# Fused attention and gated MLP: clamping converted weights on GpSimd in the opening, with a reordered opening list

## The chip, the cores and the metric

The kernel runs on one core of one Trainium2 chip. The metric is device time in microseconds (us) of one execution; the number for a version is the median of several runs.

## The reference

Eight batches with eight heads, 576 rows, head width 64 and 32 memory slots go through an attention with a compressed memory. The 4608 x 512 result then goes through a gated MLP with 1536 hidden columns.

```python
a = exp(phi - max(phi, axis=2)); a = a / (sum(a, axis=2) + 1e-09)      # over the sequence
k_m = einsum('bhsm,bhsd->bhmd', a, k);  v_m = einsum('bhsm,bhsd->bhmd', a, v)
scores = scale * matmul(q, k_m^T);  attn = softmax(scores)            # over 32 slots
x = matmul(attn, v_m), heads side by side                             # 4608 x 512
out = (sigmoid(x @ w_gate) * (x @ w_val)) @ w_out
```

All three weights reach the kernel as 64-bit words of double precision numbers, and the kernel makes float32 of them itself.

## The kernel before

**Tiling.** The attention output x is never built. For each batch b and each of 12 hidden tiles f (128 columns of gate and of value), `u b f` multiplies the small memory `vT` by the weights of the tile, and `gate b f c` multiplies the result by the attention `at` of the batch. The halves c of a batch's sequence are 256 and 320 rows. `sig`, `mul` and the split into a high and a low part follow, and `out b f c` multiplies by w_out into four accumulators. Tiles f below 3 of batch 0 are plain float32, all other products take three float32r terms.

**Stages.** The work is a list of steps. The first twelve, batches 0, 1 and 2 with f from 0 to 3, are the opening; they also hold everything that must happen before the first gate. They are written out by hand as the string `OPENING`. Steps 12 and on run in loops that the change doesn't touch.

**What the list fixes.** `step` runs one task of the list, and `queued` puts what it issues on TensorE, VectorE, ScalarE and GpSimd behind the preceding task's instructions on the same engine. So the list is the issue order of each of these four queues. DMAs of the list go to SyncE's queue (SP) in list order, by `move`; only the writes of `leave` go to GpSimd's queue. An instruction that waits holds up all that is behind it on its engine.

**Tasks of the list.** `phi b`, `kvt b`, `kvm b g`, `q b c`, `words f k r` are loads (r is the room that takes the words; k=3 is a whole gate and value tile of 1 MB, k=0 and k=1 are its halves, k=2 is a w_out tile of 512 KB). `amax`, `aexp`, `asum` are the softmax over the sequence. The calls of `mem b` walk through twelve stages in order, whatever their second number is: transposes of g 0, copy, transposes of g 1, copy, transpose of the tail, copies, products with the keys and values of g 0 and of g 1, scaling, transposes, copy to `kT`, copy to `vT`. `scores`, `blocks`, `smax`, `sub`, `sexp`, `nsum`, `nmul`, `across`, `upper`, `lower` make the attention `at` in a high and a low part. `uhi`, `ulo`, `ghi`, `glo`, `wohi`, `wolo` split operands. `warm n` issues n products that nobody reads. `keep`, `again` store and reload `at`; `leave` moves out an accumulator.

**Conversion of the weights.** `mag f k` (line L267) lets ScalarE take the absolute value of the high words. `bits f k` then holds VectorE's four instructions: a clamp between TINY and HUGE (L273), a shift with a mask (L276), and two that put sign, exponent and low bits in (L280, L285). For k=3 each of the four has its own call of `bits`; for the others the first call holds two instructions and the second two. The opening has 14 such conversions, seven of 128x1024 elements and seven of 128x512. `table_of[0]` is set during the opening and None afterwards.

```python
nc.scalar.activation(dst, words_of[f, k][:, :, 1].bitcast(F32), AF.Abs)                  # mag
...
nc.vector.tensor_scalar(dst, dst, TINY, HUGE, op0=ALU.max, op1=ALU.min)                  # bits
if k == 3:
    yield
```

A room of `words` comes free at the last instruction of its `bits`, so that instruction releases the next load into it, and with it all that is behind this load in SP's queue. `phi 2` takes the buffer of `phi 0`.

Of the kernel before, what the change touches and what calls it, by code (L numbers as in the profile page):

```python
# [13 lines left out]
ALU = mybir.AluOpType  # L14
# [21 lines left out]
TINY, HUGE = 2.0**-15, 122879.9921875  # L36
# [22 lines left out]
nmul 0 1; sig 0 1 0; mem 1 6; bits 2 3; across 0 1; mem 2 2; mem 1 7; sig 0 0 0; words 3 2 1; bits 2 3;
gate 0 0 1; mul 0 1 0; bits 2 3; mem 1 8; sig 0 0 1; mag 0 2; q 1 1; mul 0 0 0; bits 0 2; u 0 2;  # L60
mem 1 10; bits 1 2; mem 1 9; scores 1 0; nospread; uhi 0 0 2; scores 1 1; words 3 3 2; mul 0 0 1;
gate 0 1 1; kvm 2 0; sig 0 1 1; uhi 0 1 2; blocks 1 0; mag 3 2; bits 0 2; bits 1 2; ghi 0 0 1; upper 0;
mag 3 3; blocks 1 1; wohi 1; smax 1; out 0 0 0; gate 0 2 1; words 2 2 0; bits 3 3; sub 1; bits 3 3;
sig 0 2 1; mem 2 0; gate 0 2 0; gleft 0 0 1; bits 3 3; mul 0 2 1; mem 2 5; kvm 2 1; mul 0 1 1;
sig 0 2 0; out 0 1 0; bits 3 3; out 0 0 1; mul 0 2 0; kvt 2; sexp 1; nsum 1; u 0 3; gleft 0 1 1;
ghi 0 1 1; nmul 1; mem 2 6; mem 2 11; ghi 0 2 1; uhi 0 0 3; out 0 1 1; uhi 0 1 3; ulo 0 0 3; across 1;
mem 2 7; mag 2 2; upper 1; lower 0; mem 2 8; ulo 0 1 3; lower 1; bits 2 2; bits 2 2; mem 2 10;
bits 3 2; wohi 0; gate 0 3 1; gate 0 3 0; gleft 0 2 1; u 1 0 1; q 2 0; mem 2 9; sig 0 3 1; out 0 2 0;
sig 0 3 0; scores 2 0; uhi 1 0 0 1; q 2 1; keep 0; out 0 2 1; mul 0 3 1; uhi 1 1 0 1; ulo 1 0 0 1;
bits 3 2; ulo 1 1 0 1; mul 0 3 0; wohi 3; scores 2 1; u 1 2 3; kvm 3 1; blocks 2 0; gleft 0 3 1;  # L70
ghi 0 3 0; gate 1 0 1; glo 0 3 0; wolo 3; kvm 3 0; ghi 0 3 1; blocks 2 1; glo 0 3 1; gate 1 0 0;
out 0 3 1; uhi 1 0 2 3; smax 2; words 4 3 0; sig 1 0 1; mul 1 0 1; sub 2; wolo 0; ghi 1 0 1; sig 1 0 0;
uhi 1 1 2 3; sexp 2; mul 1 0 0; gleft 1 0 1; leave 0 2; gate 1 1 1; wohi 2; gate 1 1 0; ulo 1 0 2 3;
ulo 1 1 2 3; ghi 1 0 0; nsum 2; glo 1 0 1; gate 1 3 0; sig 1 1 1; glo 1 0 0; sig 1 1 0; wolo 1;
mul 1 1 0; leave 0 3; sig 1 3 0; out 0 3 0; ghi 1 1 0; out 1 0 1; mul 1 1 1; gate 1 2 1; nmul 2;
ghi 1 1 1; mag 4 3; gleft 1 1 1; gate 1 2 0; leave 0 0; sig 1 2 1; again 0; bits 4 3; out 1 0 0;
words 4 2 2; leave 0 1; mag 4 2; glo 1 1 0; glo 1 1 1; across 2; bits 4 3; mul 1 2 1; ghi 1 2 1;
u 2 0 1; sig 1 2 0; uhi 2 0 0 1; keep 1; u 2 2 3; out 1 1 0; wolo 2; phi 3; mul 1 3 0; mul 1 2 0;
uhi 2 1 0 1; gate 1 3 1; ghi 1 2 0; bits 4 3; ulo 2 0 0 1; glo 1 2 1; upper 2; ulo 2 1 0 1; bits 4 3;
out 1 1 1; glo 1 2 0; bits 4 2; sig 1 3 1; lower 2; gleft 1 2 1; out 1 2 1; words 5 3 0; uhi 2 0 2 3;  # L80
mul 1 3 1; ulo 2 0 2 3; ghi 1 3 1; gate 2 0 1; bits 4 2; ghi 1 3 0; sig 2 0 1; glo 1 3 0; gate 2 0 0;
mag 5 3; glo 1 3 1; sig 2 0 0; mul 2 0 1; amax 3; out 1 2 0; mul 2 0 0; kvt 3; bits 5 3; bits 5 3;
bits 5 3; uhi 2 1 2 3; gate 2 1 0; ghi 2 0 1; gleft 2 0 1; ghi 2 0 0; out 1 3 1; out 1 3 0; glo 2 0 0;
words 6 3 1; ulo 2 1 2 3; sig 2 1 0; bits 5 3; gleft 1 3 1; mag 6 3; wohi 4; gate 2 3 1; gate 2 2 0;
bits 6 3; bits 6 3; gate 2 1 1; sig 2 3 1; wolo 4; mul 2 1 0; leave 1 0; words 7 3 0; leave 1 1;
mul 2 3 1; keep 2; leave 1 3; ghi 2 1 0; glo 2 0 1; sig 2 2 0; sig 2 1 1; out 2 0 0; glo 2 1 0;
leave 1 2; bits 6 3; mul 2 1 1; u 0 4 5; mul 2 2 0; aexp 3 0; out 2 1 0; ghi 2 2 0; bits 6 3; mag 7 3;
gleft 2 1 1; glo 2 2 0; gate 2 3 0; gate 2 2 1; bits 7 3; out 2 0 1; uhi 0 0 4 5; ulo 0 0 4 5;
ghi 2 1 1; glo 2 1 1; words 5 2 2; aexp 3 1; ghi 2 3 1; sig 2 3 0; bits 7 3; words 6 2 3; asum 3;
bits 7 3; uhi 0 1 4 5; mul 2 3 0; sig 2 2 1; bits 7 3; ghi 2 3 0; mul 2 2 1; glo 2 3 1; ghi 2 2 1;  # L90
words 7 2 0; out 2 2 0; gleft 2 3 1; glo 2 3 0; ulo 0 1 4 5; words 8 0 1; gleft 2 2 1; glo 2 2 1;
# [12 lines left out]
def attn_moe_kernel(  # L104
# [35 lines left out]
    def att(shape, name, bufs=1):  # L140
        return sb.tile(shape, F32, name=name, bufs=bufs)
# [15 lines left out]
    table_of = [AF.Exp]  # L157
# [761 lines left out]
    def half_of(name, do):  # L919
# [714 lines left out]
```

## Time and profile before

| what | us |
|---|---|
| median of 3 runs | 711.33 |
| the three runs | 710.57 to 711.77 |
| time of the profiled execution | 711.23 |
| its span, first to last instruction | 709.4 |
| busy in the span: TensorE / VectorE / ScalarE / GpSimd | 698.7 / 554.2 / 444.2 / 27.8 |

The profiled execution lies within the runs; 1.8 us of its time are outside the span. PE is TensorE, PEld its weight loads, DVE is VectorE, ACT is ScalarE, POOL is GpSimd, SPq is SyncE's queue. A row of a timeline gives start, duration, engine, line, operation, out<-in, and in brackets the idle time of the engine ahead of it and what ended that.

### The profile page before, as it was taken

How to read it: one execution, taken by the hardware profiler on the slowest of the kernel's cores; microseconds unless marked ns; L12 is line 12 of the kernel's file. 1: busy time of each engine (PE TensorE's matmuls, PEld its weight loads, DVE VectorE, ACT ScalarE, POOL GpSimd, SP SyncE). 2: the span in 40 equal slices, each digit the busy share in tenths (PEclk: the TensorE clock that was granted, in tenths of full speed). 3: DMA queues.
4: the chain of work that ended last, by engine and by line, in shares of the span. 5: the costliest groups of instructions: out<-in, count | busy, mean ns of one | idle time of the engine just before them, and what ended most of it. 6: DMA issues, size and time to landing. Idle time of an engine off the chain costs nothing.

```text
span 709.4 us, 14029 instructions
## 1 busy us (share of the span) xinstructions
PE 698.7 (98%) x5399; PEld 576.4 (81%) x5399; DVE 554.2 (78%) x1108; ACT 444.2 (63%) x1033; POOL 27.8 (4%) x55
## 2 busy tenths in 40 slices
PE   8899999999999999999999999999999999999997
PEld 6566898888988888888888888888888888888886
DVE  4999998778787676588887779887797778987663
ACT  4675757543354454467877667865777667786553
POOL 0000100111101110100000000000000000000000
PEclk9999999999999999999999999999999999999999
DMA  8966858778975635742147313562224422151102
GB/s 341 410 240 225 343 174 331 262 257 273 328 243 175 241 106 204 242 142 91 60 158 234 141 61 114 165 252 82 101 72 142 146 79 74 62 177 60 61 1 74
DMA packets 44402, 123.19 MB, mean 174 GB/s; under 512 B 9072, under 2 KB 20976, under 8 KB 37168
## 3 DMA queue, kind: packets, MB, share of 16 engines
q1 hardware_dynamic: 39616, 106.71, 43.4%
q0 software_dynamic: 4560, 15.47, 6.2%
q8 instruction: 42, 0.69, 0.4%
q14 instruction: 24, 0.20, 0.1%
q10 hardware_dynamic: 160, 0.13, 0.1%
HBM read 96.73 MB, written 25.56 MB: 172 GB/s over the span
## 4 chain that ended last, share of the span: by engine, by line
PE 93%; DVE 3%; DMA 2%; issue 1%; ACT 1%; SPq 0%; DVEq 0%; ACTq 0%
PE acc L194 39%; PE pu_t L194 20%; PE c L194 11%; PE b L194 8%; PE a L194 8%; PE d L194 7%; DMA q<-in_qT_dram 1%; DMA ph<-in_phiT_dram 1%; DVE wg L285 0%; DVE mx L523 0%; DVE zs L538 0%; ACT ph L169 0%; DVE e L516 0%; DVE left L285 0%; DVE q L578 0%
## 5 line engine op out<-in xcount | busy, mean ns | idle before, releaser
L194 PE MATMUL acc<-wo_hi,g_hi 128*128 128x512 f32 x372 | 150.9, 406 | 0.0
L194 PE MATMUL acc<-wo_hi,g_lo 128*128 128x512 f32 x372 | 146.9, 395 | 0.0
L194 PE MATMUL acc<-wo_lo,g_hi 128*128 128x512 f32 x372 | 146.6, 394 | 0.0
L194 PE MATMUL pu_t<-at,u_hi 128*128 128x320 f32 (+1 forms) x560 | 116.5, 304 | 0.8 <-DVE at L184 0.8
L194 PEld LDWEIGHTS pu_t<-at,u_hi 128*128 128x128 f32 x560 | 92.1, 188 | 8.7 <-issue 1.9
L194 PEld LDWEIGHTS acc<-wo_hi,g_hi 128*128 128x128 f32 x372 | 69.8, 188 | 28.4 <-issue 12.3
L194 PEld LDWEIGHTS acc<-wo_hi,g_lo 128*128 128x128 f32 x372 | 69.8, 188 | 17.3
L194 PE MATMUL pu_t<-at,u_lo 128*128 128x256 f32 (+1 forms) x264 | 77.5, 293 | 0.0
L194 PEld LDWEIGHTS acc<-wo_lo,g_hi 128*128 128x128 f32 x372 | 70.0, 188 | 5.4
L1201 ACT COPY c_p<-c 128x288 f32<-128x288 f32 x60 | 24.0, 399 | 60.4 <-PE c L194 60.0
L169 ACT ACTIVATE sg<-pu_t 128x256 f32<-128x256 f32 (+1 forms) x70 | 28.6, 412 | 47.8 <-PE pu_t L194 40.4
L725 ACT CAST g_hi<-sg 128x256 fp32r<-128x256 f32 x66 | 26.4, 405 | 37.5 <-DVE sg L715 36.5
L1205 DVE TENSOR_TENSOR z<-a,c_s 128x288 f32<-128x288 f32 x60 | 27.1, 452 | 29.0 <-PE a L194 27.4
L1217 ACT CAST g_hi<-z 128x512 fp32r<-128x512 f32 x60 | 37.4, 623 | 19.6 <-DVE z L1212 19.4
L194 PEld LDWEIGHTS pu_t<-at,u_lo 128*128 128x128 f32 x264 | 49.5, 188 | 0.0
L169 ACT ACTIVATE z<-z 128x288 f32<-128x288 f32 x120 | 47.9, 441 | 1.5 <-DVE z L1205 0.8
L715 DVE TENSOR_TENSOR sg<-pu_t,sg 128x320 f32<-128x320 f32 (+1 forms) x69 | 31.0, 454 | 22.8 <-ACT sg L169 13.2
L1205 DVE TENSOR_TENSOR z<-c,c_x 128x288 f32<-128x288 f32 x60 | 27.3, 455 | 25.4 <-PE c L194 22.2
L184 DVE TENSOR_TENSOR g_lo<-z,g_hi 128x512 fp32r<-128x512 f32 x60 | 41.1, 685 | 3.6 <-ACT g_hi L1217 3.5
L194 PE MATMUL a<-ring,vT 64*32 64x512 f32 x232 | 31.4, 601 | 0.0
L194 PE MATMUL c<-ring,vT 64*32 64x512 f32 x232 | 31.4, 601 | 0.0
L184 DVE TENSOR_TENSOR g_lo<-sg,g_hi 128x256 fp32r<-128x256 f32 x66 | 26.9, 416 | 5.0 <-ACT g_hi L725 4.9
(247 smaller groups left out, 1620.7 us busy)
## 6 DMA issues: line engine op xcount, KB each, us to landing
ring<-wgv SPq DMA_DIRECT2D x30, 1024.0 KB, 4.9
kvm<-in_kvm_dram SPq DMA_DIRECT2D x14, 1024.0 KB, 9.6
at<-at SPq DMA_DIRECT2D x18, 576.0 KB, 7.7
q<-in_qT_dram SPq DMA_DIRECT2D x16, 512.0 KB, 5.8
part<-row POOLq DMA_DIRECT2D x24, 256.0 KB, 6.1
row<-part SPq DMA_DIRECT2D x24, 256.0 KB, 4.0
words<-in_wo_dram SPq DMA_DIRECT2D x8, 512.0 KB, 8.5
words<-in_wgv_dram SPq DMA_DIRECT2D x4, 1024.0 KB, 5.8
```

Of the source, the lines that this page charges most:

```text
L169: last_act[0] = nc.scalar.activation(*args, **kw)
L184: return nc.vector.tensor_tensor(lo, x, hi.bitcast(F32), op=ALU.subtract)
L194: last_pe[0] = do(*args, **kw)
L715: last_prod[0] = nc.vector.tensor_tensor(prod, ps[1][:, :n], sg[:, :n], op=ALU.mult)
L725: nc.scalar.copy(hi, prod[:, : 2 * P])
L1201: copy(getattr(self, name), self.c if name == "p5" else self.d)
L1205: nc.vector.tensor_tensor(self.z[:, i], x, y, op=ALU.add)
L1217: nc.scalar.copy(self.g[0], self.z[:, 2:4, : 2 * P])
```

## The change

Directly behind the absolute value, `magnitude` now clamps: on GpSimd in the opening (while `table_of[0]` is set), on VectorE afterwards. The minimum comes first and the maximum second. `bits_of` no longer clamps, so for k=3 its first call issues nothing. The list holds the same 401 tasks in another order; the three `warm` tasks behind the first have 33, 6 and 4 products in place of 40, 3 and 2. The part of both lists up to the first gates with three terms:

```diff
-phi 1; words 0 0 0; phi 0; table; kvt 0; amax 0; aexp 0 0; words 0 1 1; aexp 0 1; warm 46; mem 0 0;
-words 1 3 2; mag 0 0; mag 0 1; kvm 0 0; mem 0 2; mag 1 3; bits 0 1; bits 0 0; mem 0 4; mem 0 5;
-mem 0 3; amax 1; aexp 1 1; asum 0; mem 0 1; bits 1 3; warm 40; mem 0 11; aexp 1 0; bits 0 1; kvm 0 1;
-bits 1 3; warm 3; mem 0 6; phi 2; mem 0 7; bits 0 0; mem 1 5; bits 1 3; mem 0 8; mem 0 9; q 0 0;
-asum 1; bits 1 3; amax 2; q 0 1; mem 1 3; mem 0 10; aexp 2 0; scores 0 0; blocks 0 0; smax 0 0;
-scores 0 1; aexp 2 1; mem 1 0; mem 2 1; u 0 1; sub 0 0; mem 1 4; sexp 0 0; mem 1 2; uhi 0 0 1; mem 1 1;
-blocks 0 1; mem 2 3; kvm 1 0; kvt 1; u 0 0; uhi 0 1 1; words 2 3 2; uhi 0 0 0; mem 1 11; nsum 0 0;
-words 1 2 3; kvm 1 1; smax 0 1; q 1 0; nmul 0 0; mem 2 4; sub 0 1; uhi 0 1 0; sexp 0 1; mag 2 3;
-across 0 0; warm 2; gate 0 1 0; asum 2; nsum 0 1; gate 0 0 0; words 0 2 2; mag 1 2; bits 2 3;
-nmul 0 1; sig 0 1 0; mem 1 6; bits 2 3; across 0 1; mem 2 2; mem 1 7; sig 0 0 0; words 3 2 1; bits 2 3;
-gate 0 0 1; mul 0 1 0; bits 2 3; mem 1 8; sig 0 0 1; mag 0 2; q 1 1; mul 0 0 0; bits 0 2; u 0 2;
-mem 1 10; bits 1 2; mem 1 9; scores 1 0; nospread; uhi 0 0 2; scores 1 1; words 3 3 2; mul 0 0 1;
-gate 0 1 1; kvm 2 0; sig 0 1 1; uhi 0 1 2; blocks 1 0; mag 3 2; bits 0 2; bits 1 2; ghi 0 0 1; upper 0;
-mag 3 3; blocks 1 1; wohi 1; smax 1; out 0 0 0; gate 0 2 1; words 2 2 0; bits 3 3; sub 1; bits 3 3;
-sig 0 2 1; mem 2 0; gate 0 2 0; gleft 0 0 1; bits 3 3; mul 0 2 1; mem 2 5; kvm 2 1; mul 0 1 1;
-sig 0 2 0; out 0 1 0; bits 3 3; out 0 0 1; mul 0 2 0; kvt 2; sexp 1; nsum 1; u 0 3; gleft 0 1 1;
-ghi 0 1 1; nmul 1; mem 2 6; mem 2 11; ghi 0 2 1; uhi 0 0 3; out 0 1 1; uhi 0 1 3; ulo 0 0 3; across 1;
-mem 2 7; mag 2 2; upper 1; lower 0; mem 2 8; ulo 0 1 3; lower 1; bits 2 2; bits 2 2; mem 2 10;
-bits 3 2; wohi 0; gate 0 3 1; gate 0 3 0; gleft 0 2 1; u 1 0 1; q 2 0; mem 2 9; sig 0 3 1; out 0 2 0;
...
+words 0 0 0; phi 0; table; mag 0 0; words 1 3 2; phi 1; amax 0; words 0 1 1; aexp 0 1; aexp 0 0; kvm 0 0;
+warm 46; mem 0 0; mag 1 3; bits 1 3; bits 0 0; mem 0 2; kvt 0; amax 1; kvm 0 1; phi 2; mem 0 4;
+mem 0 5; mem 0 3; aexp 1 1; bits 1 3; asum 0; mag 0 1; aexp 1 0; bits 0 0; warm 33; mem 1 5; mem 1 3;
+bits 0 1; mem 0 1; bits 0 1; mem 0 11; q 0 0; warm 6; mem 0 6; mem 0 7; asum 1; mem 0 8; q 0 1;
+bits 1 3; amax 2; mem 0 9; scores 0 0; mem 0 10; u 0 0; bits 1 3; uhi 0 0 0; mem 1 0; aexp 2 0;
+scores 0 1; mem 1 4; blocks 0 0; smax 0 0; sub 0 0; kvt 1; kvm 1 0; u 0 1; sexp 0 0; aexp 2 1; mem 1 2;
+words 2 3 2; kvm 1 1; uhi 0 0 1; blocks 0 1; uhi 0 1 0; nsum 0 0; mem 1 1; mem 2 1; warm 4; mem 1 11;
+mem 2 3; smax 0 1; uhi 0 1 1; nmul 0 0; words 2 2 0; q 1 0; across 0 0; sub 0 1; mag 2 3; sexp 0 1;
+asum 2; mem 2 4; gate 0 0 0; nsum 0 1; nmul 0 1; words 0 2 2; bits 2 3; gate 0 1 0; mem 2 2; mem 1 6;
+sig 0 0 0; mem 1 7; bits 2 3; q 1 1; mem 2 0; words 1 2 3; mag 2 2; across 0 1; gate 0 0 1; bits 2 3;
+sig 0 0 1; bits 2 3; sig 0 1 0; mul 0 0 0; mag 0 2; mem 2 5; mem 1 8; mem 1 10; u 0 2; mem 1 9;
+scores 1 0; mul 0 1 0; uhi 0 0 2; words 3 3 2; nospread; scores 1 1; bits 0 2; mul 0 0 1; ghi 0 0 1;
+gate 0 1 1; uhi 0 1 2; blocks 1 0; sig 0 1 1; bits 0 2; upper 0; blocks 1 1; gate 0 2 0; bits 2 2;
+out 0 0 0; smax 1; gate 0 2 1; kvm 2 1; mag 1 2; kvm 2 0; mag 3 3; bits 3 3; sub 1; sig 0 2 0;
+mul 0 1 1; kvt 2; gleft 0 0 1; out 0 0 1; bits 1 2; lower 0; mul 0 2 0; mem 2 6; mem 2 11; bits 3 3;
+sig 0 2 1; mul 0 2 1; bits 3 3; sexp 1; u 1 0 1; words 3 2 1; bits 3 3; bits 1 2; mem 2 7; gleft 0 1 1;
+u 0 3; gleft 0 2 1; uhi 0 0 3; nsum 1; out 0 1 0; uhi 0 1 3; nmul 1; ghi 0 1 1; across 1; mag 3 2;
+ulo 0 1 3; ulo 0 0 3; uhi 1 0 0 1; ulo 1 0 0 1; upper 1; out 0 1 1; gate 0 3 0; gate 0 3 1; lower 1;
+mem 2 8; sig 0 3 1; bits 2 2; bits 3 2; ghi 0 2 1; mem 2 10; wohi 0; bits 3 2; out 0 2 0; sig 0 3 0;
...
@@ in magnitude
         nc.scalar.activation(dst, words_of[f, k][:, :, 1].bitcast(F32), AF.Abs)
+        clamp = nc.gpsimd if table_of[0] is not None else nc.vector
+        clamp.tensor_scalar(dst, dst, HUGE, TINY, op0=ALU.min, op1=ALU.max)
@@ in bits_of
-        nc.vector.tensor_scalar(dst, dst, TINY, HUGE, op0=ALU.max, op1=ALU.min)
```

## Rows read from the trace of the kernel before

**Rows 1.** The page's first part: busy us, share, instructions of each engine.

```profile
PE 698.7 (98%) x5399; PEld 576.4 (81%) x5399; DVE 554.2 (78%) x1108; ACT 444.2 (63%) x1033; POOL 27.8 (4%) x55
```

**Rows 2.** Busy time by stretch: length, five engines, granted clock, DMA share, GB/s.

```profile
0.00:10.06 10.06, 6.96 (x47) 5.34 (x47) 1.69 (x3) 2.41 (x5) 0.70 (x6) 1.00 0.81 280
10.06:22.11 12.05, 10.14 (x140) 7.94 (x141) 9.99 (x18) 8.06 (x18) 0.00 (x0) 1.00 1.02 417
22.11:35.41 13.30, 12.16 (x191) 8.33 (x191) 12.02 (x26) 9.49 (x20) 0.00 (x0) 0.87 1.01 410
35.41:57.69 22.28, 21.45 (x223) 13.38 (x219) 21.97 (x34) 15.30 (x33) 0.00 (x0) 1.00 0.49 193
57.69:117.80 60.11, 60.11 (x441) 48.43 (x442) 57.70 (x100) 39.77 (x87) 4.89 (x8) 1.00 0.77 283
117.80:709.40 591.60, 587.84 (x4364) 492.97 (x4362) 450.88 (x930) 369.19 (x872) 22.20 (x41) 1.00 0.45 150
```

**Rows 3.** Timeline of PE in the opening.

```profile
10.06 1.52 PE L194 MATMUL pu_t<-ident,ph 128*128 128x128 f32 x9 [1.74 <-ACT ph L169]
...
17.73 1.08 PE L194 MATMUL pu_t<-kvm,row 128*32 128x128 f32 x32
...
22.11 0.60 PE L194 MATMUL acc<-q,kT 64*32 64x256 f32 x1 [1.68 <-DMA q<-in_qT_dram]
...
29.22 0.38 PE L194 MATMUL acc<-ident 128*128 128x256 bf16 x2
30.56 3.69 PE L194 MATMUL acc<-at,u_hi 128*128 128x256 f32 x16 [0.96 <-DVE at L581]
...
56.46 0.39 PE L194 MATMUL pu_t<-at,u_hi 128*128 128x320 f32 x1
57.69 0.41 PE L194 MATMUL pu_t<-at,u_hi 128*128 128x320 f32 x1 [0.83 <-DVE at L184]
...
60.91 1.09 PE L194 MATMUL pu_t<-wg,vT 64*32 64x512 f32 x16
```

**Rows 4.** Timeline of all engines around the first softmax load.

```profile
1.20 0.41 SPq L180 DMA_DIRECT2D words<-in_wgv_dram  x1
...
8.29 1.41 DVE L381 TENSOR_REDUCE nmx<-ph 128x1 f32<-128x576 f32 x2 [7.15 <-DMA ph<-in_phiT_dram]
```

**Rows 5.** That load of words: KB, us from issue to landing.

```profile
words<-in_wgv_dram SPq DMA_DIRECT2D x1, 512.0 KB, 5.5
```

**Rows 6.** Timeline of DVE and ACT in the opening.

```profile
29.25 0.82 DVE L525 TENSOR_TENSOR e<-e,mx 128x640 f32<-128x640 f32 x1
29.98 0.76 DVE L581 STREAM_TRANSPOSE at<-e 128x256 f32<-128x256 f32 x2
30.10 0.74 ACT L169 ACTIVATE e<-e 128x640 f32<-128x640 f32 x1 [1.05 <-DVE e L525]
30.74 1.14 ACT L267 ACTIVATE wg<-wg 128x1024 f32<-128x1024 f32 x1
34.02 0.90 DVE L581 STREAM_TRANSPOSE at<-e 128x320 f32<-128x320 f32 x2
39.84 0.77 DVE L516 STREAM_TRANSPOSE e<-acc 128x256 f32<-128x256 f32 x2
57.55 0.41 DVE L184 TENSOR_TENSOR u_lo<-pu_t,u_hi 128x256 fp32r<-128x256 f32 x1
```

**Rows 7.** DVE in the opening, grouped by line and shape: count, busy us, mean ns.

```profile
L273 DVE TENSOR_SCALAR wg<-wg 128x1024 f32<-128x1024 f32 x7 | 4.8, 679 | 0.3 <-ACT wg L267 0.3
...
L273 DVE TENSOR_SCALAR left<-left 128x512 f32<-128x512 f32 x3 | 1.3, 424 | 0.0
```

**Rows 8.** POOL's groups in the whole run, same columns.

```profile
masks.py:199 POOL TENSOR_SCALAR_AFFINE_SELECT ident<-ident 128x128 f32<-128x128 f32 x1 | 0.3, 287 | 0.1
masks.py:197 POOL MEMSET ident<- 128x128 f32 x1 | 0.2, 206 | 0.3 <-POOLq L1624 0.3
L1624 POOL MEMSET const-bfloat16-1.0<- 128x1 bf16 x1 | 0.1, 101 | 0.0
```

More of the change, by code (lines that the diff above doesn't have):

```diff
@@ L66 @@
-ghi 0 1 1; nmul 1; mem 2 6; mem 2 11; ghi 0 2 1; uhi 0 0 3; out 0 1 1; uhi 0 1 3; ulo 0 0 3; across 1;
-mem 2 7; mag 2 2; upper 1; lower 0; mem 2 8; ulo 0 1 3; lower 1; bits 2 2; bits 2 2; mem 2 10;
-bits 3 2; wohi 0; gate 0 3 1; gate 0 3 0; gleft 0 2 1; u 1 0 1; q 2 0; mem 2 9; sig 0 3 1; out 0 2 0;
-sig 0 3 0; scores 2 0; uhi 1 0 0 1; q 2 1; keep 0; out 0 2 1; mul 0 3 1; uhi 1 1 0 1; ulo 1 0 0 1;
-bits 3 2; ulo 1 1 0 1; mul 0 3 0; wohi 3; scores 2 1; u 1 2 3; kvm 3 1; blocks 2 0; gleft 0 3 1;
@@ L71 @@
[L71 to L91, printed above, removed]
@@ L92 @@
-out 2 1 1
+words 0 0 0; phi 0; table; mag 0 0; words 1 3 2; phi 1; amax 0; words 0 1 1; aexp 0 1; aexp 0 0; kvm 0 0;
[3 more added lines that the diff above has]
+bits 1 3; amax 2; mem 0 9; scores 0 0; mem 0 10; u 0 0; bits 1 3; uhi 0 0 0; mem 1 0; aexp 2 0;
@@ new lines @@
+u 0 3; gleft 0 2 1; uhi 0 0 3; nsum 1; out 0 1 0; uhi 0 1 3; nmul 1; ghi 0 1 1; across 1; mag 3 2;
+ulo 0 1 3; ulo 0 0 3; uhi 1 0 0 1; ulo 1 0 0 1; upper 1; out 0 1 1; gate 0 3 0; gate 0 3 1; lower 1;
+mem 2 8; sig 0 3 1; bits 2 2; bits 3 2; ghi 0 2 1; mem 2 10; wohi 0; bits 3 2; out 0 2 0; sig 0 3 0;
+q 2 0; mul 0 3 0; wohi 1; wolo 0; wohi 2; mul 0 3 1; uhi 1 1 0 1; gleft 0 3 1; ulo 1 1 0 1; q 2 1;
+wohi 3; mem 2 9; kvt 3; wolo 3; out 0 2 1; words 4 2 2; scores 2 0; scores 2 1; blocks 2 0; gate 1 0 1;
@@ new lines @@
+gate 1 0 0; blocks 2 1; wolo 1; ghi 0 3 0; ghi 0 3 1; sig 1 0 1; smax 2; u 1 2 3; words 4 3 0; mag 4 2;
+gate 1 1 0; glo 0 3 0; sig 1 0 0; uhi 1 0 2 3; mul 1 0 1; uhi 1 1 2 3; sub 2; phi 3; mul 1 0 0;
+kvm 3 1; out 0 3 0; sexp 2; ghi 1 0 0; glo 0 3 1; ulo 1 0 2 3; gleft 1 0 1; mag 4 3; ghi 1 0 1;
+ulo 1 1 2 3; gate 1 1 1; amax 3; wolo 2; out 0 3 1; sig 1 1 1; glo 1 0 0; gate 1 2 0; keep 1; nsum 2;
+leave 0 0; mul 1 1 1; gate 1 2 1; gate 1 3 0; leave 0 3; sig 1 1 0; gleft 1 1 1; glo 1 0 1; bits 4 3;
@@ new lines @@
+out 1 0 1; mul 1 1 0; ghi 1 1 1; glo 1 1 1; ghi 1 1 0; sig 1 2 1; nmul 2; leave 0 2; glo 1 1 0;
+out 1 0 0; u 2 0 1; across 2; u 2 2 3; sig 1 2 0; mul 1 2 1; leave 0 1; out 1 1 0; bits 4 3; sig 1 3 0;
+out 1 1 1; mul 1 2 0; mul 1 3 0; upper 2; gate 1 3 1; ghi 1 2 0; uhi 2 0 0 1; bits 4 2;
+bits 4 3; aexp 3 1; bits 4 3; uhi 2 1 0 1; glo 1 2 0; ulo 2 0 0 1; keep 0; ulo 2 1 0 1; lower 2;
+ghi 1 2 1; aexp 3 0; out 1 2 0; bits 4 2; gleft 1 2 1; glo 1 2 1; ghi 1 3 0; sig 1 3 1; words 5 3 0;
+words 6 3 1; uhi 2 0 2 3; ulo 2 0 2 3; uhi 2 1 2 3; glo 1 3 0; mul 1 3 1; gate 2 1 0; mag 5 3;
@@ new lines @@
+out 1 3 0; leave 1 0; ulo 2 1 2 3; ghi 1 3 1; gate 2 0 0; sig 2 0 0; gate 2 2 1; mul 2 0 0; glo 1 3 1;
+ghi 2 0 0; bits 5 3; asum 3; bits 5 3; gate 2 1 1; glo 2 0 0; sig 2 1 0; gleft 1 3 1; sig 2 2 1;
+mul 2 1 0; bits 5 3; gate 2 0 1; sig 2 1 1; bits 5 3; mul 2 2 1; mag 6 3; bits 6 3; ghi 2 1 0; wohi 4;
+out 1 2 1; bits 6 3; glo 2 1 0; mul 2 1 1; wolo 4; sig 2 0 1; words 7 3 0; mul 2 0 1; gleft 2 0 1;
+out 1 3 1; gate 2 2 0; ghi 2 1 1; gleft 2 2 1; gate 2 3 1; leave 1 1; bits 6 3; glo 2 1 1; leave 1 3;
@@ L93 @@
+leave 1 2; gleft 2 1 1; ghi 2 0 1; sig 2 3 1; mag 7 3; bits 6 3; glo 2 0 1; sig 2 2 0; again 0;
+out 2 0 0; mul 2 3 1; mul 2 2 0; u 0 4 5; ghi 2 2 0; gate 2 3 0; bits 7 3; uhi 0 0 4 5; sig 2 3 0;
+words 5 2 2; words 6 2 3; uhi 0 1 4 5; glo 2 2 0; out 2 0 1; bits 7 3; bits 7 3; mul 2 3 0; ghi 2 3 0;
+keep 2; ghi 2 3 1; ghi 2 2 1; kvm 3 0; bits 7 3; ulo 0 0 4 5; out 2 1 0; glo 2 3 0; ulo 0 1 4 5;
+glo 2 3 1; out 2 1 1; words 7 2 0; words 8 0 1; out 2 2 0; glo 2 2 1; gleft 2 3 1
 """
```

## The prediction

> **What bounds the kernel now.** I read the page's busy shares first: PE is busy for 698.7 of 709.4 us [rows 1]. A busy PE is no proof of a full PE, so the next view is the busy time by stretch, cut where PE's work changes character [rows 2]. Four things are to be seen there. Up to 22.11 us DMA runs at 0.81 and then 1.02 of its engines, and PE fills its time with products that nobody reads. From 22.11 to 35.41 DMA is still full and PE's clock is granted at 0.87 on average. From 35.41 to 57.69 DMA falls to 0.49, and DVE is busy for 21.97 of 22.28 us. From 57.69 on PE is busy all the time to 117.80, where the listed opening ends, and nearly so afterwards, in code that the change leaves alone but for the order of two clamps. So the change can move the end only by what PE loses ahead of 117.8 us, and each loss has its own cause.
>
> The timeline of PE names them [rows 3]. The first transposes at 10.06 wait for ScalarE's exponential of `phi`. The first scores at 22.11 wait for a DMA, the load of `q`. The first gate at 30.56 waits 0.96 us for DVE's `across`, although PE was done with all else at 29.22 + 0.38 = 29.60. The first gate with three terms begins at 56.46 and stands until 57.69, again for DVE: 57.69 - 56.46 less a step of about 0.2 is some 1.0 to 1.2 us. That is what the change has to work on.
>
> **What leaves DVE and what comes to POOL.** The opening's 14 clamps cost DVE 7 x 0.679 + 7 x 0.424 = 7.7 us [rows 7]; the wide ones are seven, and the row of three stands for the seven narrow ones, which differ by the buffer alone. Between the first scores and the gate with three terms the new list has five of the 14 behind `mag` (2 3, 2 2, 0 2, 1 2, 3 3): 2 x 0.68 + 3 x 0.42 = 2.6 us of DVE at most. The rest leaves DVE where it had nothing to wait for, before 22.11, or where PE doesn't wait for it, after 57.69; the latter costs nothing as long as PE has products in hand, which it has for all of the 60.11 us [rows 2].
>
> POOL's price for a clamp stands nowhere in the trace. The nearest rows are its fill of 128x128 in 0.206 us, its triangular select over the same size, which reads as well as writes, in 0.287, and a fill of one column in 0.101 [rows 8]. Per column that is (206 - 101)/127 = 0.83 ns and (287 - 101)/127 = 1.46 ns; a narrow clamp lies between 0.5 and 0.85 us, a wide one between 0.95 and 1.6. I take the upper ends, since a clamp reads and writes. POOL has nothing else to do before the first `leave`, and that is later than 70 us in both lists, so no clamp queues behind a transfer in the stretch that counts.
>
> **The start.** The new list loads `words 0 0 0` and `phi 0` first and `phi 1` later. In the old list the second transfer, 512 KB, is issued at 1.20 and lands 5.5 us later, at 6.7 [rows 4, 5], and `phi 0`, the third, releases DVE at 8.29 [rows 4]. As second, with about the same bytes ahead of it, `phi 0` would land at 6.7. But `aexp 0 1` now comes before `aexp 0 0`, and it needs the second maximum; then the exponential that the first transposes need starts near 6.7 + 1.45 + 0.8 = 9.0, against 9.1 before. They gain about 0.1 us, and that ends in `warm`. The products with the keys (17.73) and the scores (22.11) wait for transfers [rows 3], and up to `kvm 0 1`, and again up to `q 0 0`, both lists load the same bytes. With DMA full, 22.11 stays. The absolute values and clamps that moved here are covered by that wait.
>
> **To the first gate.** From the scores on DVE's chain is `blocks`, `smax`, `sub`, `nsum`, `nmul`, `across`. The old list has `sub 0 1` ahead of `across 0 0`: 29.98 - 29.25 = 0.73 us [rows 6]. The new one has it behind. The set of PE's tasks ahead of the first gate is the same but for two more `warm` products, so PE would be ready near 29.60 + 0.2 = 29.8. The gate starts 0.58 us after `across` now (30.56 - 29.98), so it would start at 29.98 - 0.73 + 0.58 = 29.83: a gain of 0.7.
>
> **What gives it back.** `mag 2 3`, 1.14 us [rows 6], now stands ahead of `sexp 0 1` on ScalarE. I place it at 29.85, behind the copies that precede it, so the exponential starts at 31.0, not at 30.10. The clamp that left DVE there (0.6) makes good part of these 0.9: `across 0 1` would start at 34.4, not at 34.02 [rows 6]. Its gate was held by PE at 35.41, not by `across`, so at 34.4 + 0.58 = 35.0 it is still 0.4 early. Then the copy to `kT`, which the scores of batch 1 need, stands behind `mag 0 2` and two copies more on ScalarE and ends near 38.7, as in the old run; I count the gain there as zero. `bits 0 2` also has to wait for its clamp: `mag 0 2` ends near 37.75, POOL adds 0.85, and DVE, done by 38.1, waits some 0.5 us for it.
>
> **To the gate with three terms.** From `blocks 1 0` to the last `ulo` of f 3, DVE's tasks sum to about the same in both lists: 19.1 us of durations before, 19.3 after (`bits 2 2` and `lower 0` change places with clamps and shifts). The old one takes from 39.84 to 57.55 + 0.41, 18.1 us [rows 6]; the new one should take 18.2. It starts at 39.4, from the walk above, and ends at 57.6. PE gets there at about 56.9, waits for the third term, and has done both halves, 60.91 - 57.69 = 3.2 us of products [rows 3] less some that ran during the wait, at 60.65. The old run is there at 60.91, with other work behind it: the new list has by then done `u 1 0 1`, 1.02 us, and not yet the transposes of `mem 2`, 0.36. The sum is (60.91 + 1.02 - 0.36) - 60.65 = 0.9 us. From there on PE has the same products in either list and doesn't wait. So the profiled execution would go from 711.23 to **710.3 us**. It lies 0.1 below the median of the runs, 711.33, so the two can be taken for each other. A difference below 0.2%, 1.4 us, can't be told from no change with this kernel.
>
> **Rivals.**
>
> *POOL and DVE hold each other up (slower).* Nothing in this trace can show it: POOL computes only in the first 1.3 us. If an instruction of DVE stands while POOL clamps, the four clamps between 35 and 57 us can cost DVE up to 3 x 0.85 + 1.6 = 4.15 us, and there DVE leads. All of it would make 710.3 + 4.15 = 714.4; half of it, since some of DVE's work there is transposes, reductions and products out of PSUM, 712.4. It decides from 0.9 + 1.4 = 2.3 us of blocking. The place where I would look first is `clamp 3 3` over `sub 1` and the shift behind it. The Trainium skill (SBUF — State Buffer, "Who interferes with whom") states such a rule: DVE instructions with two inputs in SBUF, or in a mode that uses two ports, and GpSimd instructions shut each other out for a whole instruction, whoever starts first. By that rule the time is between 712.4 and 714.4, without it the sum stays at 710.3; no run so far bears on it.
>
> *DVE's lead vanishes (faster).* If POOL's clamps run beside DVE and ScalarE's order costs less than I placed it at, PE loses neither wait: 0.96 at the first gate and 1.2 at 57.69, and some 0.4 of the slower start of the scores of batch 0, whose stretch ran at a granted clock of 0.87 [rows 2]. That is 2.5 us and gives 708.7. For it: DVE is busy all the time there, so each clamp that goes counts. Against it: `sexp 0 1` and `kT`.
>
> *The clock.* The stretch from 22.11 to 35.41 loses 13.3 x 0.13 = 1.7 us by the granted clock [rows 2], after an idle wait of 1.68 [rows 3]. The wait stays, so I leave the loss as it is; without it the case above is reached, at 710.3 - 1.7 = 708.6.
>
> *It is hidden.* Up to 22.11 DMA decides, after 57.69 PE does, and what DVE saves between is given back to ScalarE's order: 711.2.
>
> **How the numbers follow.** Forecast (710.3, own range 709.8 to 711.0) 0.35; DVE's lead vanishes, or the clock stays up, 0.33; hidden 0.13; POOL and DVE hold each other up 0.19, of which 0.16 cost over 2.3 us and 0.03 less. Faster by over 0.2% is the second case, 0.33; slower 0.16; the rest, 0.51, lies within. The range takes the middle of the fast case and most of the slow one, and the narrow clamps' lower price (0.5) lies inside it: 708.3 to 713.0.
>
> **What would show it.** The first scores near 22.1, after a wait for `q`; an earlier wait than that refutes the start. The first gate near 29.8. `sexp 0 1` behind an absolute value, near 31.0. The scores of batch 1 near 38.7. DVE's wait ahead of `bits 0 2`. The first gate with three terms some 0.9 us ahead by equal work, and the last listed product at 116.9 in place of 117.8. POOL's clamps should take 0.5 to 0.85 and 0.95 to 1.6 us; longer ones, or DVE's L276 and L280 standing idle while they run, make it wrong, as would a PE that waits after 60 us.

## The result and the profile after

The changed kernel takes 719.94 us (median of 4 runs, 719.67 to 720.42) where the kernel before takes 711.41 in the same comparison (4 runs, 710.57 to 711.77). The ratio is 1.0127, 95% interval 1.0115 to 1.0140. The forecast, 710.3, and its range, up to 713.0, both missed. The profiled execution took 720.00 us with a span of 718.1.

The page's first part for the changed kernel, which answers to [rows 1]:

```profile
PE 700.7 (98%) x5397; PEld 578.6 (81%) x5397; DVE 549.7 (77%) x1094; ACT 444.6 (62%) x1033; POOL 41.4 (6%) x69
```

DVE has 14 instructions fewer and POOL 14 more, as the change says. PE is busy for 2.0 us longer, so most of the 8.7 us by which the span grew is time in which PE stands. Busy time by stretch shows where (columns as in [rows 2]):

```profile
10.06:22.39 12.33, 9.34 (x136) 7.23 (x134) 8.41 (x14) 6.15 (x15) 1.65 (x2) 1.00 1.03 414
22.39:34.59 12.20, 11.08 (x194) 8.18 (x195) 10.97 (x24) 9.47 (x22) 1.04 (x1) 1.00 0.98 387
34.59:57.48 22.89, 22.09 (x229) 13.51 (x229) 22.42 (x33) 14.21 (x33) 5.09 (x5) 1.00 0.54 211
57.48:117.48 60.00, 59.87 (x430) 48.98 (x431) 54.60 (x92) 41.12 (x88) 10.11 (x13) 1.00 0.71 263
117.48:162.00 44.52, 44.52 (x371) 37.84 (x370) 31.74 (x63) 22.58 (x55) 6.00 (x11) 1.00 0.69 255
162.00:167.10 5.10, 0.82 (x5) 0.34 (x3) 1.35 (x3) 1.34 (x3) 1.08 (x2) 1.00 0.73 217
167.10:173.90 6.80, 4.69 (x16) 4.40 (x17) 2.65 (x5) 0.44 (x1) 1.09 (x2) 0.50 0.99 378
173.90:718.10 544.20, 540.33 (x3977) 452.23 (x3976) 415.55 (x859) 345.19 (x813) 14.07 (x26) 1.00 0.41 138
```

The opening's last product ends at 117.48, 0.3 us ahead of 117.80 before. The loss lies 45 us behind it, in code that neither the diff nor the list touches: from the opening's end to the end of the span it is 718.1 - 117.48 = 600.6 us against 591.6 [rows 2], 9.0 more. Of these PE stands for 6.4 us from 162.8 on, and its clock is granted at 0.50 (1.2 GHz) from 167.10 to 173.90. There it is busy for 4.69 us and does what takes half of that at the full clock, which is 2.3 us lost. The two make 8.7 of the 9.0 us. The timeline of PE, in the opening (compare [rows 3]) and around the wait:

```profile
9.82 1.20 PE L193 MATMUL pu_t<-ident,ph 128*128 128x128 f32 x9 [0.67 <-ACT ph L168]
...
22.39 0.40 PE L193 MATMUL acc<-q,kT 64*32 64x256 f32 x1 [0.46 <-ACT kT L470]
...
29.16 0.45 PE L193 MATMUL acc<-at,u_hi 128*128 128x256 f32 x1
...
34.59 2.39 PE L193 MATMUL pu_t<-at,u_hi 128*128 128x320 f32 x8 [0.25 <-DVE at L581]
...
57.48 0.50 PE L193 MATMUL pu_t<-at,u_hi 128*128 128x256 f32 x2 [0.67 <-DVE u_lo L183]
...
60.85 0.60 PE L193 MATMUL pu_t<-ident,row 128*128 128x128 f32 x4
...
162.42 0.40 PE L193 MATMUL acc<-wo_hi,g_lo 128*128 128x512 f32 x1
169.21 0.80 PE L193 MATMUL acc<-wo_hi,g_hi 128*128 128x512 f32 x1 [6.40 <-DVE row L775]
```

The line named, L775, is the addition in `leave` that frees an accumulator of batch 0's second group of four tiles (f 4 to 7). DVE's timeline shows that it waits for a transfer, the read-back of a partial result:

```profile
168.47 0.69 DVE L775 TENSOR_TENSOR row<-acc,row 128x512 f32<-128x512 f32 x1 [3.59 <-DMA row<-part]
```

So SP's timeline is the next view. These are its read-backs between 95 and 176 us in the changed kernel (start of the first, time until the last of the group is issued):

```profile
98.27 0.33 SPq L179 DMA_DIRECT2D row<-part  x1
135.90 27.35 SPq L179 DMA_DIRECT2D row<-part  x4
```

and in the kernel before:

```profile
136.49 3.40 SPq L180 DMA_DIRECT2D row<-part  x4
```

Before, four read-backs go out within 3.4 us. After, one more stands alone at 98.27, and the group of four takes 27.35 us: its last read-back goes out only at 162.9. The issues of the changed kernel around 98.3 and around 163 give 2.6 us to landing for the one and 5.4 for the other (KB, us from issue to landing):

```profile
row<-part SPq DMA_DIRECT2D x1, 256.0 KB, 2.6
...
row<-part SPq DMA_DIRECT2D x1, 256.0 KB, 5.4
```

The lone read-back comes from a rule in `out_half`, whose text is the same in both kernels:

```python
if (b, f + 1) in ends and c:
    for t in range(SF):
        if (b, t) in part and (b, t) not in rows:
            rows[b, t] = row_of(b, t)
```

`ends` holds the last tile of each group of four, f 3, 7 and 11. So one tile ahead of such an end, in its second half, the rule reads back every partial row of its batch that is already written. `out 1 2 1` meets the condition. In the old list `leave 1 0` stands behind it, so nothing of batch 1 is written yet; in the new list `leave 1 0` stands ahead of it, and the row just written is read back at once. It isn't needed before the end of batch 1's second group: where it is read with the others (first experiment), that happens at 176.00. Until then it holds one of the four `row` buffers (`bufs=4` in `row_of`). Batch 0's fourth read-back then finds no buffer until the write of another row, issued at 158.10, has landed 4.8 us later, at 162.9. SP's waits between 130 and 165 us show it (us in total, times, longest); the same view of the kernel before lists no wait for such a write:

```profile
SPq L179 <- DMA part<-row: 25.4, 3, 24.5
```

### The profile page after: what moved, and what is told of

The parts are those of the page before. It is cut to its first block, busy times and chain, and to the rows that moved or that the text cites. A ratio compares the mean times of both kernels' runs of the same rounds, so it can differ in the third digit from the quotient of the medians.

```text
span 718.1 us, 14027 instructions
## 1 busy us (share of the span) xinstructions
PE 700.7 (98%) x5397; PEld 578.6 (81%) x5397; DVE 549.7 (77%) x1094; ACT 444.6 (62%) x1033; POOL 41.4 (6%) x69
## 4 chain that ended last, share of the span: by engine, by line
PE 88%; DMA 4%; DVE 4%; ACT 2%; issue 1%; POOL 0%; SPq 0%; DVEq 0%; ACTq 0%
PE acc L193 37%; PE pu_t L193 18%; PE c L193 11%; PE b L193 8%; PE a L193 7%; PE d L193 7%; DMA ph<-in_phiT_dram 2%; DMA wg<-in_wgv_dram 1%; DMA row<-part 1%; DMA part<-row 1%; DVE wg L285 1%; ACT wg L266 0%; DVE nmx L381 0%; ACT L163 0%; DVE e L544 0%
## 5 line engine op out<-in xcount | busy, mean ns | idle before, releaser
L1217 ACT CAST g_hi<-z 128x512 fp32r<-128x512 f32 x60 | 37.4, 623 | 19.3 <-DVE z L1212 19.1
```

Source lines behind the costliest of these rows:

```text
L1217: nc.scalar.copy(self.g[0], self.z[:, 2:4, : 2 * P])
```

## Experiments: where the loss comes from

The theory: the place of `leave 1 0` ahead of `out 1 2 1` costs all of it, through the row buffer. The rivals: POOL's clamps hold DVE up, or the new order loses the time in another way.

**The corrected list.** `leave 1 0` is moved behind `out 1 2 1`, and nothing else.

```diff
-out 1 3 0; leave 1 0; ulo 2 1 2 3; ghi 1 3 1; gate 2 0 0; ...
+out 1 3 0; ulo 2 1 2 3; ghi 1 3 1; gate 2 0 0; ...
...
-out 1 2 1; bits 6 3; ...
+out 1 2 1; leave 1 0; bits 6 3; ...
```

> The changed kernel with one task moved: leave 1 0 stands behind out 1 2 1 instead of ahead of it. Theory A (row buffer): out 1 2 1 reads back the partial row of batch 1, tile 0, when that has been written out before; it then holds one of four row buffers from 98 us on, and the fourth read-back of batch 0 waits for a buffer until 162.9 us. Without it the wait of 6.4 us of TensorE near 162 us and the half clock from 167 to 174 us go, all read-backs of batch 0 are issued near 136 to 140 us, and the time is 710.5 to 711.3. Theory B (GpSimd's clamps delay its queue's writes, or hold VectorE up, and that is what comes out late): nothing changes, 719 to 720.5.

Measured: 710.88 us (11 runs) against 711.12, ratio 0.9999, 0.9990 to 1.0008. SP's timeline has the four read-backs together again, with no lone one, and the same stretches as above show PE busy throughout at the full clock:

```profile
135.98 2.80 SPq L179 DMA_DIRECT2D row<-part  x4
...
176.00 2.78 SPq L179 DMA_DIRECT2D row<-part  x4
```

```profile
162.00:167.10 5.10, 5.10 (x31) 4.58 (x30) 4.34 (x9) 2.23 (x6) 1.61 (x3) 1.00 0.74 242
167.10:173.90 6.80, 6.80 (x64) 5.06 (x62) 5.57 (x12) 2.48 (x7) 0.55 (x1) 1.00 1.01 302
```

One task moved by three lines of the list takes away the whole loss. It doesn't say yet that the read-back is the reason, since the task's DVE and POOL work moved as well.

**The changed list without the read-back.** The list stays as changed; `out_half` doesn't read back while the list runs.

```diff
-if (b, f + 1) in ends and c:
+if (b, f + 1) in ends and c and not later:
```

> The changed kernel with its whole order, leave 1 0 ahead of out 1 2 1 too, but out_half reads no partial row back while the list runs. Theory A (the read-back holds a row buffer): as with the task moved, 710.4 to 711.4, no wait of TensorE above 1 us behind 118 us. Theory C (the place of leave 1 0 itself, its write in GpSimd's queue, does it): 719 to 720.5.

Measured: 710.87 us (10 runs) against 711.28, ratio 0.9998, 0.9989 to 1.0007. `leave 1 0` stands where the change put it, and the loss is gone: SP's four read-backs stand together, and no wait of PE is listed behind 60 us. So it is the read-back and not the place of the `leave`.

```profile
136.13 2.90 SPq L179 DMA_DIRECT2D row<-part  x4
```

**The held buffer alone, in the kernel before.** One line behind the loop over the list of the kernel before:

```diff
+rows[1, 0] = row_of(1, 0)
```

> The kernel before with the read-back of batch 1, tile 0 behind the last task of the list, so that it stands in nobody's way inside the opening and only holds a row buffer. Theory A: the opening ends at 117.8 us as before, then TensorE waits 6 to 7 us near 163 us and runs at half clock behind it; 8 to 9 us above before, 719 to 720.5. If the earlier run of 728 was due to something else than the buffer: 711 to 712.

Measured: 720.34 us (4 runs) against 711.28, ratio 1.0128, 1.0114 to 1.0142. One early read-back, with the old list and the clamps on DVE, gives the size of the whole loss. The row has landed 6.1 us after its issue at 117.10, so by 136 us nothing is left of it but the buffer that it holds. PE's waits and SP's read-backs are those of the changed kernel:

```profile
PE acc L194 <- DVE row L775: 6.3, 1, 6.3
```

```profile
117.10 0.35 SPq L180 DMA_DIRECT2D row<-part  x1
136.58 27.42 SPq L180 DMA_DIRECT2D row<-part  x4
```

**The read-back at the old place of the `leave`.** In the kernel before, the row (1, 0) is read back right behind its write.

```diff
+if (b, t) == (1, 0):
+    rows[b, t] = row_of(b, t)
```

> The kernel before with the early read-back alone: directly behind leave 1 0 the row of batch 1, tile 0 is read back; no clamp and no order is changed. Theory A: one of four row buffers is held from about 105 us on, TensorE waits 5 to 7 us near 162 us, its clock falls to half behind it, 718.5 to 721. Theory B: 711.0 to 711.8, as before.

Measured: 727.90 us (4 runs) against 711.12, ratio 1.0231, 1.0217 to 1.0245: more than the changed kernel, and above the range expected. The profiled execution was the shortest of the four, 726.12. PE's waits behind 60 us show the same 6.3 and a new one of 4.6 in the opening:

```profile
PE acc L194 <- DVE row L775: 6.3, 1, 6.3
PE pu_t L194 <- DVE u_lo L184: 4.6, 1, 4.6
```

SP stands for 13.4 us ahead of the read-back, which waits for its row's write to land. In the old list the four `leave` of batch 1 follow within a few tasks, so the held buffer is missed there as well: DVE's fourth copy waits 2.59 us for one. The loads of words behind the read-back come late, ScalarE's absolute value waits 3.93 us for one of them, and the opening ends at 124.21. So two costs add up here: the held buffer, with the same 6.3 us as before, and in the opening the time for which SP's queue and a buffer are taken. The price of an early read-back depends on who stands behind it; no run separates queue and buffer in the opening.

## Experiments: what the change itself does

**The clamps alone.** The kernel before with its old list, and the clamps on GpSimd.

```diff
 nc.scalar.activation(dst, words_of[f, k][:, :, 1].bitcast(F32), AF.Abs)
+clamp = nc.gpsimd if table_of[0] is not None else nc.vector
+clamp.tensor_scalar(dst, dst, HUGE, TINY, op0=ALU.min, op1=ALU.max)
...
-nc.vector.tensor_scalar(dst, dst, TINY, HUGE, op0=ALU.max, op1=ALU.min)
```

> The kernel before with the clamps moved to GpSimd, minimum first, and the old order of the list. Theory A with the forecast's sum: VectorE loses 7.7 us of work in the opening and its wait ahead of the first three-term gate at 57.69 us shrinks by up to 1.0 us; 710.3 to 711.4. Rival (the two engines shut each other out): VectorE's instructions with two inputs from SBUF stand while GpSimd clamps, that gate comes 1 us or more later, 712.4 to 714.4.

Measured: 711.92 us (11 runs) against 711.12, ratio 1.0013, 1.0004 to 1.0022. Neither of the expected ranges has it. The gate with three terms goes on at 57.83 where it goes on at 57.69 before [rows 3]: DVE has less to do and isn't earlier. Its timeline says why: four of its instructions, each beside a clamp, take 1.41, 1.09, 1.93 and 1.48 us, where the kernel before has 0.81, 0.69, 1.35 and 1.32. The 1.7 us more take back most of the 2.2 that VectorE's four clamps took in this stretch of the kernel before.

```profile
32.31 1.41 DVE L545 TENSOR_TENSOR e<-e,zs 128x640 f32<-128x640 f32 x1
33.64 1.09 DVE L277 TENSOR_SCALAR wg<-wg 128x1024 int32<-128x1024 int32 x1
...
45.36 1.93 DVE L526 TENSOR_TENSOR e<-e,mx 128x1152 f32<-128x1152 f32 x1
...
56.29 1.48 DVE L184 TENSOR_TENSOR at<-at 128x1152 fp32r<-128x1152 f32 x1
```

**The order alone.** The corrected list, with the clamps back on DVE in `bits`.

```diff
-clamp = nc.gpsimd if table_of[0] is not None else nc.vector
-clamp.tensor_scalar(dst, dst, HUGE, TINY, op0=ALU.min, op1=ALU.max)
...
+nc.vector.tensor_scalar(dst, dst, TINY, HUGE, op0=ALU.max, op1=ALU.min)
```

> The new order with leave 1 0 behind out 1 2 1, and the clamps back on VectorE in bits. If the clamps' removal from VectorE is what the new order lives on, VectorE gets 2.6 us more to do ahead of the three-term gate and that comes 1.5 to 2.6 us later: 712.3 to 713.8. If the order alone sets the time: 710.5 to 711.5.

Measured: 714.51 us (4 runs) against 711.12, ratio 1.0047, 1.0033 to 1.0061, above the range expected. Its scores start at 24.13, its opening ends at 121.59, and PE waits longer for DVE at the gate with three terms, in its timeline:

```profile
60.44 0.50 PE L193 MATMUL pu_t<-at,u_hi 128*128 128x256 f32 x2 [1.30 <-DVE u_lo L183]
```

So the new order costs 3.4 us with the clamps on VectorE, and the clamps on GpSimd pay nothing in the old order; together, with `leave 1 0` put right, they come out at 0.9999.

**No clamps at all in the list.** The corrected list without the clamps of the 14 weights that it converts.

```diff
-clamp.tensor_scalar(dst, dst, HUGE, TINY, op0=ALU.min, op1=ALU.max)
+if clamp is nc.vector:
+    clamp.tensor_scalar(dst, dst, HUGE, TINY, op0=ALU.min, op1=ALU.max)
```

> The mended kernel without any clamp in the opening: the clamp of the 14 weights of the list is left out of the computation. It gives the whole price that GpSimd's clamps still have. If they hold VectorE up or are waited for: 0.5 to 2 us below the mended kernel, 709 to 710.4. If they are free: 710.6 to 711.2.

Measured: 710.24 us (11 runs) against 711.28, ratio 0.9988, 0.9979 to 0.9997. That is about 0.8 us (0.11%) less than the corrected list, and an estimate of the most that a better placing of these clamps could give with this list. The profiled execution was the longest of its 11, 711.71, and its clock was granted at 0.50 early on:

```profile
21.40:28.20 6.80, 6.34 (x90) 3.10 (x89) 4.93 (x9) 3.93 (x12) 0.00 (x0) 0.50 0.99 377
```

Its first gate starts at 30.85, against 29.21 in the corrected list's run with the clock at 1.00 there, and its gate with three terms at 58.18 against 57.36. Between the two it makes good 1.64 - 0.82 = 0.8 us, of which up to 0.73 - 0.21 = 0.5 is PE's shorter wait for the last `ulo`.

**Every clamp of the list twice.** The corrected list, with a second instruction like the first on GpSimd.

```diff
 clamp.tensor_scalar(dst, dst, HUGE, TINY, op0=ALU.min, op1=ALU.max)
+if clamp is nc.gpsimd:
+    clamp.tensor_scalar(dst, dst, HUGE, TINY, op0=ALU.min, op1=ALU.max)
```

> The mended kernel (leave 1 0 behind out 1 2 1) with every clamp on GpSimd done twice, one behind the other. If GpSimd's clamps stand in VectorE's way, or their length counts, another 0.6 and 1.0 us each on GpSimd cost as much again as the first set: 711.5 to 713.5. If they run beside VectorE and are awaited by nobody: 710.7 to 711.3.

Measured: 715.04 us (4 runs) against 711.28, ratio 1.0054, 1.0040 to 1.0069. The second set costs (1.0054 - 0.9999) x 711 = 3.9 us, more than the expected range allows. Not all of it is VectorE's standing: PE's wait at the gate with three terms is 1.71 us and not 0.73, and behind it the clock is granted at 0.50 from 62 to 65 us in the profiled run. DVE waits 1.11 us for POOL ahead of a shift, and instructions of both engines are shown longer where they meet. POOL's and DVE's timelines of this kernel:

```profile
31.60 1.04 POOL L270 TENSOR_SCALAR wg<-wg 128x1024 f32<-128x1024 f32 x1
...
45.43 2.14 POOL L268 TENSOR_SCALAR wg<-wg 128x1024 f32<-128x1024 f32 x1
47.65 1.09 POOL L270 TENSOR_SCALAR wg<-wg 128x1024 f32<-128x1024 f32 x1
```

```profile
31.91 0.76 DVE L541 TENSOR_SCALAR zs<-zs 128x20 f32<-128x20 f32 x1
...
44.94 1.73 DVE L527 TENSOR_TENSOR e<-e,mx 128x1152 f32<-128x1152 f32 x1
...
47.77 2.18 DVE L183 TENSOR_TENSOR at<-at 128x1152 fp32r<-128x1152 f32 x1
```

Read as a lock, each length follows from the other engine. DVE's last one comes at 47.77 while POOL clamps until 47.65 + 1.09 = 48.74; alone it takes 1.34 (the changed kernel's `at<-at` at 46.02), and 48.74 + 1.34 = 50.08, against an end shown at 47.77 + 2.18 = 49.95. POOL's clamp at 45.43 comes while DVE works until 44.94 + 1.73 = 46.67; 46.67 + 1.04 = 47.71, against 47.57. Both agree to 0.14 us. The short addition to the sums at 31.91, with one input, stands as well: 0.18 us without a clamp (31.94 in the corrected list's run), and 31.60 + 1.04 + 0.18 = 32.82 against 32.67. The one that comes second stands until the first is done, in both directions.

**The exponential first.** A test of that reading where it can be told beforehand: in the corrected list `sexp 0 1` goes ahead of `mag 2 3`, so that the clamp falls on DVE's product with the reciprocals.

```diff
-sub 0 1; mag 2 3; sexp 0 1;
+sub 0 1; sexp 0 1; mag 2 3;
```

> The corrected list (`leave 1 0` behind `out 1 2 1`) with `sexp 0 1` ahead of `mag 2 3` on ScalarE. In the corrected list's run the exponential started at 30.32 and VectorE waited 0.71 us for it at 31.08; here it should start at 30.1, VectorE's sum near 30.9 and its product with the reciprocals (128x640, alone 0.82 us) near 32.3. `mag 2 3` then runs to about 31.9 and GpSimd's clamp of 128x1024 from about 32.0 to 33.05. If an instruction of VectorE with two inputs in SBUF stands while GpSimd clamps, the product is shown with about 1.4 to 1.5 us instead of 0.82, `across 0 1` begins near 34.2 (33.81 there) and its gate near 34.9 (34.46 there). If the two only slow each other a little or not at all, the product takes 0.8 to 1.0, `across 0 1` begins near 33.6 and the gate near 34.4, where TensorE is done with all else. In the time neither can be told from the kernel before: 710.7 to 711.5, ratio 0.999 to 1.001.

Measured: 711.35 us (10 runs) against 711.13, ratio 1.0006, 0.9996 to 1.0015. POOL's, DVE's and PE's timelines:

```profile
32.01 1.04 POOL L268 TENSOR_SCALAR wg<-wg 128x1024 f32<-128x1024 f32 x1 [16.64 <-ACT wg L266]
```

```profile
32.31 1.42 DVE L544 TENSOR_TENSOR e<-e,zs 128x640 f32<-128x640 f32 x1
...
34.25 0.89 DVE L581 STREAM_TRANSPOSE at<-e 128x320 f32<-128x320 f32 x2
```

```profile
34.89 1.32 PE L193 MATMUL pu_t<-at,u_hi 128*128 128x320 f32 x4 [0.47 <-DVE at L581]
```

The product stands until 32.01 + 1.04 = 33.05, and 33.05 + 0.82 = 33.87, against an end shown at 33.73. Its 1.42 us, 34.25 for `across 0 1` and 34.89 for the gate are the numbers of the lock. What ScalarE gained was lost to it, and the order that looked better isn't: its time can't be told from the kernel before, as expected.

No version measured here beats the kernel before by more than its measurement can tell, except the one that leaves out the clamps.

## Why the prediction was wrong, step by step

**The failed step** is the last of the sum: "From there on PE has the same products in either list and doesn't wait". The products are the same; the wait of 6.4 us isn't. The prediction compared the two lists task by task up to the gate with three terms and took the 60 to 118 us behind it, and all that follows, as one block with PE busy. There the lists differ in the order of `leave 1 0` and `out 1 2 1`, and `out_half` asks what has been written when it issues its read-backs. The change thus moved a DMA and the hold on a buffer, though no line of that code was edited. "A PE that waits after 60 us" was named as what would make the forecast wrong, without a place or a price. It cost 719.94 - 710.88 = 9.1 us, ten times the 0.9 that the sum came to, and no rival reached it: the slowest of them ended at 714.4. Both removals (0.9999 and 0.9998) and the addition to the kernel before (1.0128) show it.

**The rest of the sum** can be judged on the changed kernel up to 117.48 and on the corrected list beyond it.
- *The start* was right in its ends and not in its waits: DVE's first maximum starts at 6.64 (6.7 forecast), the first transposes come 0.24 earlier (0.1), the scores at 22.39 (22.1). The wait ahead of the scores was misnamed: it is ScalarE's copy to `kT`, 0.46 us, not the load of `q`, and 1.17 us of waiting moved ahead, to the load of `kvm` at 19.23. The prediction had named an earlier wait as what would refute this step.
- *The clock* stayed up: 1.00 from 22.39 to 34.59, against 0.87 in [rows 2]. The prediction gave this a place among the rivals and not in the sum. The first gate is at 29.16 and not at 29.83; in the run without clamps, where the clock fell, it is at 30.85. That rival's time, 708.6, didn't come either: in the corrected list's run the clock stays at 1.00 from 20 to 36 us, and the time is that of the kernel before.
- *ScalarE's order*: the exponential starts at 30.46 behind the absolute value (31.0 forecast), the second gate at 34.59 (35.0), the scores of batch 1 at 38.27 (38.7), each 0.4 to 0.5 early with the first gate. `across 0 1` starts at 33.94 (34.4 forecast, where its terms 34.02 + 0.9 - 0.6 give 34.3). DVE's wait ahead of `bits 0 2` didn't come.
- *POOL's price* lay inside the bounds and below the value taken: 0.61 us for 128x512 and 1.04 for 128x1024 where nothing meets it, against 0.85 and 1.6. DVE's shift L276 stood idle for a clamp once, 0.94 us at 15.31, ahead of the scores.
- *DVE's stretch to the gate with three terms* was mis-sized. From 39.06 on, the last `ulo` of f 3 ends at 57.76 (two of them in 0.72 us from 57.04), 18.7 us against 18.2 forecast (its own sums, 18.1 and 19.3 for 19.1, give 18.3). POOL and DVE hold each other up there, and just ahead of it:

```profile
35.64 0.78 POOL L268 TENSOR_SCALAR left<-left 128x512 f32<-128x512 f32 x1 [3.96 <-ACT left L266]
...
43.03 0.61 POOL L268 TENSOR_SCALAR left<-left 128x512 f32<-128x512 f32 x1 [5.06 <-ACT left L266]
44.09 1.73 POOL L268 TENSOR_SCALAR wg<-wg 128x1024 f32<-128x1024 f32 x1 [0.44 <-ACT wg L266]
54.86 1.31 POOL L268 TENSOR_SCALAR wo_raw<-wo_raw 128x512 f32<-128x512 f32 x1 [9.04 <-ACT wo_raw L266]
```

```profile
35.98 1.52 DVE L285 SCALAR_TENSOR_TENSOR wg<-wg 128x1024 int32<-128x1024 int32 x1
...
42.19 1.34 DVE L523 TENSOR_REDUCE mx<-e 128x36 f32<-128x1152 f32 x1
43.56 1.36 DVE L525 TENSOR_TENSOR e<-e,mx 128x1152 f32<-128x1152 f32 x1
...
45.24 0.86 DVE L276 TENSOR_SCALAR left<-left 128x512 int32<-128x512 int32 x1
46.02 1.34 DVE L183 TENSOR_TENSOR at<-at 128x1152 fp32r<-128x1152 f32 x1
```

The place named first in the prediction, the clamp of `mag 3 3` over `sub 1` and the shift behind it, is the one at 44.09: POOL stands until `sub 1` is done, clamps, and the shift stands for 0.86 - 0.43 = 0.43 us. That is most of the 0.5 us by which the stretch is longer. With 1.52 - 1.21 = 0.31 at 35.98 DVE loses 0.74 us between 35 and 58 us. The rival's mechanism was right and its price, half or all of 4.15, was not: 2.3 us of blocking, from which it decides, weren't reached. There were also five clamps in this time and not four: `mag 3 2`, at 54.86, stands ahead of the gate in the new list. DVE loses only where POOL began first and DVE's instruction is of a kind that stands; the maximum at 42.19 runs beside a clamp and neither is longer, and the clamps at 44.09 and 54.86 themselves stood for what they took beyond 1.04 and 0.61.
- *The sum for the opening* was a gain of 0.9 us. At equal work it was (60.91 + 1.02 - 0.36) - 60.85 = 0.7 and at 117.48 it was 0.3. So it came out smaller, although the clock gave what the forecast hadn't counted; between the two points 0.4 us go in small pieces that I didn't take apart. The corrected list ends its opening at 117.41 and its time can't be told from the kernel before: the "same" case, without the early read-back.

The Trainium skill (SBUF — State Buffer, "Who interferes with whom") gives the rule that the prediction weighed: whoever issues first has the ports for the whole instruction, and a reduction of DVE never contends on this chip. The trace agrees in both: the 1.42 us of the last experiment and the unstretched 1.34 and 0.61 around 43. How often the two meet with POOL first is for the timelines to show, and it made 0.74 us of 4.15 here; in the old order, with the clamps alone, it made 1.7.

## What to carry to other kernels

Where a list's tasks ask at issue time what has been done so far (what is written, which buffer is held), moving a task across the asking one changes which transfers are issued, far from the edited part; compare the DMA issues of the two orders and not only the compute. A read-back issued early isn't free: it holds a buffer until it is used, and its price appears at the next one who asks for that buffer, here some 40 us later. Work moved from VectorE to GpSimd didn't count in full here: behind a clamp that began first, VectorE's instructions with two inputs in SBUF, its shift and a short addition with one input waited out the rest of it. A reduction (42.19) and products out of PSUM (0.74 us for two at 37.42, beside the clamp at 37.32) weren't longer.

## What the runs showed of the hardware

- A single wait of PE cost more than its length. PE stopped at 162.8, the granted clock went to the lower level at 167.1, with PE still idle, and returned at 173.9, 4.7 us after PE had resumed; products of 0.39 to 0.40 us took 0.63 to 0.80. That is 2.3 us on top of 6.4.
- The opening's fall of the clock isn't fixed to an order: in the profiled executions it lies within 22.11 to 35.41 in the kernel before [rows 2], is missing in the changed kernel, and lasted from 21.4 to 28.2 in the profiled run without clamps, whose waits (1.29, 0.60 and 0.46 us) are nearly those of the changed kernel (1.17, 0.60 and 0.46). The run with the early read-back has the list of the kernel before up to that point and shows 1.00 from 20 to 36 us; its wait for `q` is 0.3 us there and not 1.68. What decides it in this kernel stays open.
- POOL's clamp costs (1.04 - 0.61)/512 = 0.84 ns per column of float32; two in a row start 0.69 us apart at 128x512 (6.05 and 6.74) and 1.12 at 128x1024 (30.48 and 31.60) in the run with clamps twice. It and DVE's instructions with two inputs in SBUF, its shift and its short addition shut each other out for whole instructions: the ends computed here on that reading lie within 0.15 us of those shown.
